# One of four weight products of an attention-and-MLP kernel, done by seven block products of halves

## The chip, the cores and the metric

The kernel runs on one core of one Trainium2 chip. The metric is the time of one execution on the device, in microseconds (us); smaller is better. The engines are named as in the profile: PE (TensorE, with PEld for its weight loads), DVE (VectorE), ACT (ScalarE), POOL (GpSimd) and SP (SyncE, which here issues nearly all transfers).

## The reference, cut to what matters

```python
scores = einsum('bhij,hg->bgij', scale * q @ k.T, w_pre)      # 4 batches, 12 heads, 448 rows, 64 wide
attn = softmax(scores);  attn = einsum('bhij,hg->bgij', attn, w_post)
x = (attn @ v)                                   # as 1792 tokens x 768
# first MLP:  w_in 768 x 2048, w_out 2048 x 768
h = x @ w_in;  g = relu(h) ** 2;                 x = g @ w_out
# second MLP: weights of its own, the same shapes
h = x @ w_in;  g = h * clip(h + 3, 0, 6) / 6;    out = g @ w_out
```

## The kernel before, in words

The four batches are worked off in two groups of two (`gi` 0 and 1). Each group goes through its attention and then through both MLPs, which work on the two batches at once: everything is held transposed, features along the 128 partitions and 2 x 448 tokens along the columns. `e` counts the two batches of the group.

Products are made at about full float32 accuracy out of fp32r matmuls: each operand is split in a high part (a copy in the rounded type, made by ACT) and a low part (the value less its high part), and one product is three matmuls: high by high, low weights by high data, high weights by low data. One matmul has a 128 x 128 block of weights and 448 columns of data.

An MLP is a list of units; a unit is one weight tile of 128 x 768. The 16 "h" units make the hidden values: unit `fc` gives 128 of the 2048 hidden features, for both `e`, in 2 x 18 matmuls (six blocks along the 768 features, three matmuls each). The 16 "p" units make the output in two halves (`dg` 0 and 1) of eight units, each 36 matmuls into six accumulators (three `d` of 128 features, two `e`), which stay open over the eight units. A group has thus 64 units. In the second group the weights come from DRAM (`kept`), where the first group has put them converted.

The order of the work on each engine is the order in which the program issues it; each engine works its list off in that order, and waits where an operand or a buffer is not ready. `Mlps.run` goes through the units: at the head of unit n it issues the load of unit n + 2 (SP) and `split(n + 1)`, that is `wh` of the next unit on ACT and `wl` behind it, on POOL in the second group. `wh` and `wl` have two buffers each, so `wh` of unit n + 1 needs the matmuls of unit n - 1 done. Then come the unit's matmuls. In an "h" unit `act` follows each product (for the second MLP: ACT makes `r` = relu(h/6 + 1/2), DVE makes `g` = min(r, 1) * h, both read the product where it lies), and `split_g` (ACT the high part, POOL the low part). The last of a unit's two products is taken up within the next unit: `act` before `split(n + 1)`, `split_g` behind it. At the end of the first MLP `finish` splits its output for the second: ACT makes `yh`, DVE `yl`.

PE's results lie in eight banks. In attention, and before the change in the MLPs too, they are four named tiles: `bs` and `bx`, two banks each, `bm` and `bo`, two single banks each; the allocation of this program puts `bs` in banks 0 and 1, `bx` in 2 and 3, `bm` in 4 and 5, `bo` in 6 and 7. `hidden` takes `bm`. Attention ends with `closing`, whose last products are read out of `bx` and then of `bs` (into `xr`, line 302).

The tile framework puts in the semaphore waits. Buffers with one tag take turns.

Of the kernel before, what the change touches and what calls it, by code (L numbers as in the profile page):

```python
# [7 lines left out]
F32 = mybir.dt.float32  # L8
F32R = mybir.dt.float32r
U32 = mybir.dt.uint32  # L10
I64 = mybir.dt.int64
# [26 lines left out]


# [19 lines left out]
def attention_mlp_kernel(ctx: ExitStack, tc, qT, kT, v, w_pre, w_post, mask, w1_in, w1_out, w2_in, w2_out, outT):  # L59
# [22 lines left out]
    ps = ctx.enter_context(tc.tile_pool(name="ps", bufs=2, space=PSUM))  # L82
# [372 lines left out]
    kept = {}  # L455

    class Mlps:
        def __init__(self, gi, att):
            self.gi, self.att = gi, att
            self.units = []  # L460
            for which, (w_in, w_out) in enumerate(((w1_in, w1_out), (w2_in, w2_out))):
                self.units += [("h", which, n, w_in[n]) for n in range(NF)]
                self.units += [("p", which, n, w_out[n // NU, n % NU]) for n in range(DG * NU)]
            self.W = w1_in.shape[-1]
            self.arena, self.ready, self.late, self.scaled = None, {}, [], set()
# [5 lines left out]
        def wr(self, n):  # L471
            at = 2 * 2 * self.W + self.W * (n % 3)
            return self.arena[:, at:at + self.W]

        def load(self, n):
            if n >= len(self.units):
                return
            if self.arena is None:
                self.arena = sh.tile([P, 7 * self.W], F32, tag="e1", name=f"arena{self.gi}")
            if self.gi == 0:  # L480
                nc.sync.dma_start(out=self.raw(n).bitcast(I64), in_=self.units[n][3])
            else:
                nc.sync.dma_start(out=self.wr(n), in_=kept[n])
# [71 lines left out]
        def hidden(self, which, fc, e, wh, wl):  # L555
            cols = slice(e * S, (e + 1) * S)
            hp = bank("bm", f"ps_h{self.gi}_{which}_{fc}_{e}")
# [38 lines left out]

        def opening(self):
# [6 lines left out]
        def run(self, mp, behind):  # L604

            rest = None
            for n, (kind, which, m, _) in enumerate(self.units):
# [11 lines left out]
                if kind == "p":  # L619
                    self.convert(n + 2, 1)  # L620
                wh, wl = self.ready.pop(n)
                if kind == "h":
# [23 lines left out]
                if u == 0:  # L646
# [10 lines left out]
                if m == 0 and which == 0:  # L657
                    self.yh = sh.tile([P, KC, T], F32R, tag="x1", name=f"yh{self.gi}")
                    self.yl = sh.tile([P, KC, T], F32R, tag="x2", name=f"yl{self.gi}")
                ends = u == NU - 1  # L660
                for e in range(NB):
                    self.project(u, e, wh, wl, acc)
                    if ends:
                        self.finish(which, dg, e, range(DB), acc)
                if which == 0 and m == DG * NU - 1:
# [7 lines left out]
    with tc.manual_schedule():  # L673
# [4 lines left out]
        for gi in range(groups):  # L678
# [10 lines left out]
            with tc.tile_pool(name=f"mp{gi}", bufs=1, reuse_waits="tile") as mp:  # L689
                mlp.run(mp, att.opening() + att.ahead() if att else [])  # L690
# [54 lines left out]
```

## Time and profile before

| | us |
|---|---|
| median of 3 runs | 1404.93 (1404.64 to 1406.46) |
| profiled execution, its own time | 1403.79 |
| its span, first to last instruction | 1401.9 |
| second group, first MLP, h units | about 931.3 to 1048.0 |
| second group, first MLP, p units | 1048.0 to 1165.0 |
| second group, second MLP, h units | 1165.0 to 1281.4 |
| second group, second MLP, p units | 1281.4 to the end |

The times of the stages are from the span's start. The span leaves out 1.9 us of the profiled execution's own time.

### The profile page before, as it was taken

Reading aid. Unit: us, or ns where it says so; the run is one execution under the profiler, and the core shown is the slowest. Engines: PE = TensorE matmul, PEld = TensorE weight load, DVE = VectorE, ACT = ScalarE, POOL = GpSimd, SP = SyncE. Lnnn points to the kernel's source line nnn. Section 1 sums busy time; section 2 is a strip of 40 time slices with the busy share of each in tenths; the row PEclk is TensorE's granted clock in tenths of the full one; section 3 lists DMA queues with packets and bytes.
Section 4 is the critical chain, followed back from the end, with each engine's and each line's share of the span. In section 5 each row is a group of like instructions: output and inputs, shape, how many; then the busy total and the mean of one; then the engine's idle time right before and its main releaser. Section 6 shows DMA issues by size and latency. Waiting matters only on the chain.

```text
span 1401.9 us, 22130 instructions
## 1 busy us (share of the span) xinstructions
PE 1385.5 (99%) x8500; PEld 1194.9 (85%) x8500; DVE 670.8 (48%) x1297; ACT 549.3 (39%) x1025; POOL 385.5 (27%) x431
## 2 busy tenths in 40 slices
PE   8999999999999999999999999999999999999998
PEld 3777778999989899988977777789999999999998
DVE  4777677877565687755547766741110102111000
ACT  4554445555222355524244534434431114443121
POOL 0222223344100133300012212245552224554221
PEclk9999999999999999999999999999999999999999
DMA  6453543555545455566554435311111111111121
GB/s 176 131 138 89 141 111 123 169 167 153 171 153 169 137 167 170 165 188 200 178 144 131 126 101 142 99 65 53 49 57 57 57 57 48 55 57 57 57 93 43
DMA packets 68366, 162.67 MB, mean 116 GB/s; under 512 B 6821, under 2 KB 43429, under 8 KB 68261
## 3 DMA queue, kind: packets, MB, share of 16 engines
q1 hardware_dynamic: 64805, 155.75, 38.0%
q10 hardware_dynamic: 3456, 5.51, 1.0%
q8 instruction: 67, 1.10, 0.3%
q14 instruction: 38, 0.31, 0.1%
HBM read 92.03 MB, written 30.67 MB: 88 GB/s over the span
## 4 chain that ended last, share of the span: by engine, by line
PE 95%; DVE 2%; ACT 1%; DMA 1%; issue 1%; POOL 0%; SPq 0%; ACTq 0%; POOLq 0%; DVEq 0%
PE ps_h L561 33%; PE ps_a L575 12%; PE bx L575 11%; PE ps_o L267 11%; PE bs L575 10%; PE ps_m L219 9%; PE bx L294 3%; PE bs L294 2%; PE bs L192 2%; PE bx L192 2%; DMA t<-s 0%; PE ps_s L307 0%; PE ps_s L192 0%; DVE arena L501 0%; DMA first<-in_dram 0%
## 5 line engine op out<-in xcount | busy, mean ns | idle before, releaser
L267 PEld LDWEIGHTS ps_o<-w2s,p 120*112 120x112 f32 (+1 forms) x1440 | 169.7, 177 | 70.9 <-issue 56.2
L517 ACT ACTIVATE wh<-arena 128x768 fp32r<-128x768 f32 x128 | 107.4, 839 | 294.4 <-PE bs L575 247.2
L236 ACT ACTIVATE p<-ps_m,mx 120x448 f32<-120x448 f32 x180 | 114.2, 634 | 186.2 <-DVE z L242 83.5
L519 POOL TENSOR_TENSOR wl<-arena,wh 128x768 fp32r<-128x768 f32 x64 | 118.2, 1847 | 236.3 <-ACT wh L517 233.1
L267 PE MATMUL ps_o<-w2s,p 120*112 120x120 f32 (+1 forms) x1440 | 181.2, 269 | 2.0 <-POOL w2s L256 1.8
L219 PE MATMUL ps_m<-t,w1f 120*120 120x448 f32 x360 | 168.2, 550 | 5.2 <-DMA t<-s 2.6
L256 POOL TENSOR_SCALAR w2s<-w2f,rz 120x120 f32<-120x120 f32 x180 | 66.4, 369 | 356.2 <-DVE rz L248 315.2
L553 POOL TENSOR_TENSOR gl<-g,gh 128x448 fp32r<-128x448 f32 x80 | 98.8, 1236 | 228.1 <-ACT gh L552 180.0
L561 PE MATMUL ps_h<-xh,wh 128*128 128x448 f32 x384 | 140.6, 366 | 0.0
L561 PE MATMUL ps_h<-xh,wl 128*128 128x448 f32 x384 | 140.3, 365 | 0.1
L561 PE MATMUL ps_h<-yh,wh 128*128 128x448 f32 x384 | 140.3, 365 | 0.0
L561 PE MATMUL ps_h<-yh,wl 128*128 128x448 f32 x384 | 140.2, 365 | 0.0
L561 PE MATMUL ps_h<-xl,wh 128*128 128x448 f32 x384 | 139.6, 364 | 0.1
L561 PE MATMUL ps_h<-yl,wh 128*128 128x448 f32 x384 | 139.4, 363 | 0.0
L282 DVE COPY a<-ps_o 112x480 f32<-112x480 f32 (+1 forms) x176 | 115.1, 654 | 31.8 <-PE ps_o L267 22.1
L228 DVE TENSOR_REDUCE mx<-ps_m 120x1 f32<-120x448 f32 x180 | 111.6, 620 | 23.2 <-PE ps_m L219 20.1
L519 DVE TENSOR_TENSOR wl<-arena,wh 128x768 fp32r<-128x768 f32 x64 | 62.8, 981 | 104.7 <-ACT wh L517 103.8
L575 PE MATMUL ps_a<-gh,wh 128*128 128x448 f32 x288 | 106.5, 370 | 0.0
L575 PE MATMUL ps_a<-gh,wl 128*128 128x448 f32 x288 | 104.8, 364 | 0.0
L542 DVE SCALAR_TENSOR_TENSOR g<-r,ps_h 128x448 f32<-128x448 f32 x64 | 39.7, 620 | 119.0 <-ACT r L541 115.9
L575 PE MATMUL bx<-gh,wh 128*128 128x448 f32 x256 | 93.4, 365 | 2.4 <-DVE yl L585 2.4
L575 PE MATMUL bx<-gh,wl 128*128 128x448 f32 x256 | 93.3, 364 | 0.0
(105 smaller groups left out, 2552.8 us busy)
## 6 DMA issues: line engine op xcount, KB each, us to landing
arena<-in_dram SPq DMA_DIRECT2D x64, 768.0 KB
t<-s SPq DMA_DIRECT2D x176, 210.0 KB
keep<-arena SPq DMA_DIRECT2D x64, 384.0 KB
arena<-keep SPq DMA_DIRECT2D x64, 384.0 KB
v<-in_dram SPq DMA_DIRECT2D x8, 672.0 KB
outT_dram<-ot ACTq DMA_DIRECT2D x24, 224.0 KB
kr<-in_dram SPq DMA_DIRECT2D x18, 224.0 KB
qr<-in_dram SPq DMA_DIRECT2D x30, 110.0 KB
```

The costliest lines, as they stand in the source:

```text
L219: nc.tensor.matmul(m[:rows, :S], lhsT=w1f.rearrange("p i g -> p (i g)")[:rows, :rows], rhs=self.live.pop(("t", i))[:rows], start=True, sto ...
L228: nc.vector.reduce_max(mx[:rows], m[:rows, :S], axis=AX.X, negate=True)
L236: nc.scalar.activation(pt[:rows], m[:rows, :S], AF.Exp, bias=mx[:rows], accum_out=z[:rows])
L256: nc.gpsimd.tensor_scalar(w2s[:rows, :G * ni].rearrange("p (g i) -> p g i", g=G), w2f[:rows, :, :ni], rz[:rows], 1.0, op0=ALU.mult, op1=AL ...
L267: nc.tensor.matmul(o[:JP, q * G * ni:(q + 1) * G * ni], lhsT=pt[:rows, q * JP:(q + 1) * JP], rhs=w2s[:rows, :G * ni], start=True, stop=True)
L282: nc.vector.tensor_copy(dst, src)
L294: nc.tensor.matmul(xo[e * D:(e + 1) * D, k * n:(k + 1) * n], lhsT=self.v[:, q, g, :], rhs=self.aa[c][:, q, g, :n], start=(q == 0), stop=(q ...
L517: nc.scalar.activation(wh, self.wr(n), AF.Copy)
L519: eng.tensor_tensor(out=wl, in0=self.wr(n), in1=f(wh), op=ALU.subtract)
L553: nc.gpsimd.tensor_tensor(out=gl, in0=g, in1=f(gh), op=ALU.subtract)
L561: nc.tensor.matmul(hp[:, :S], lhsT=lw[:, c * P:(c + 1) * P], rhs=rw[:, c, cols], start=(k == 0), stop=(k == 3 * KC - 1))
L575: nc.tensor.matmul(acc[d, e][:, :S], lhsT=lw[:, wc], rhs=rw[fc, e], start=(fc == 0 and k == 0), stop=(fc == NF - 1 and k == 2))
```

## The change

In the second group's second MLP the 16 "h" units are replaced by 28 "s" units. Take two hidden tiles (a "pair") as the rows, and the first and second half of the 768 features (384 each) as the columns of a 2 x 2 matrix A of weight blocks; the halves of x by the two batches `e` are the 2 x 2 matrix B. Their product is made with seven block products (the Winograd form) and sums of blocks. A product is three 128 x 128 blocks, nine matmuls, into one bank; an "s" unit holds two. Eight pairs make 56 products, worked off two pairs (14 products, seven units) at a time, in the order `PRODUCTS`. The numbers 1 to 7 name the products: 1 = A11 B11, 2 = A12 B21, 3 = S4 B22, 4 = A22 T4, 5 = S1 T1, 6 = S2 T2, 7 = S3 T3.

The sums of weights S1 to S4 are made on DVE during the first MLP's p units (`prepare`), and put into DRAM (`sums`). The sums of x, T1 to T4, and all their high and low parts are made where the first MLP's output is finished (`finish_mixed`; the branch in the diff is that of the last accumulators). Results are put together by DVE while they are read out of the banks (`combine`), and the gate follows one product later (`gate`). For hidden tiles 10 to 15 (`LATE`) the split of g is left to the first three p units (`split_late`). For this group's MLPs the four named bank tiles are closed and all eight banks become one pool `pb` that takes turns, from bank 0 on. Weight tiles from unit 16 on get three buffers of their own. `wl` of the s units and of the last p units is made by DVE instead of POOL. A scratch area in SBUF is made smaller.

```diff
+PRODUCTS = (
+    (1, 0), (1, 1), (2, 0), (2, 1), (6, 0), (7, 0), (5, 0), (4, 0), (3, 0), (6, 1), (7, 1), (5, 1), (4, 1), (3, 1),
+)
+SUMS = {6: 0, 3: 1, 7: 2, 5: 3}
+LATE = 10
...
+                if self.last and which == 1:
+                    self.base = at
+                    self.prods = [(p, 2 * j + i) for j in range(NF // 4) for p, i in PRODUCTS]
+                    self.units += [("s", which, n, None) for n in range(len(self.prods) // 2)]
...
         def load(self, n):
...
+                for i in range(2):
+                    p, pair = self.prods[2 * m + i]
+                    a = self.base + 2 * pair
+                    if p in SUMS:
+                        of = sums[pair][:, SUMS[p] * HW:(SUMS[p] + 1) * HW]
+                    else:
+                        of = kept[a + (p == 4)][:, (p > 1) * HW:(1 + (p > 1)) * HW]
+                    nc.sync.dma_start(out=self.wr(n)[:, i * HW:(i + 1) * HW], in_=of)
...
-            eng = nc.vector if self.gi == 0 else nc.gpsimd
+            eng = nc.vector if self.gi == 0 or self.last and n >= self.base else nc.gpsimd
             eng.tensor_tensor(out=wl, in0=self.wr(n), in1=f(wh), op=ALU.subtract)
...
+        def bank(self, tag, name):
+            if self.last:
+                return self.mb.tile([128, 512], F32, tag="pb", name=name, bufs=8)
...
+        def prepare(self, n):
...
+            nc.vector.tensor_tensor(out=a22, in0=a21, in1=a22, op=ALU.add)
+            nc.vector.tensor_tensor(out=a21, in0=a11, in1=a21, op=ALU.subtract)
+            nc.vector.tensor_tensor(out=a11, in0=a22, in1=a11, op=ALU.subtract)
+            nc.vector.tensor_tensor(out=a12, in0=a12, in1=a11, op=ALU.subtract)
+            sums[m] = dr.tile([P, 4 * HW], F32, name=f"sums{m}")
+            nc.sync.dma_start(out=sums[m], in_=self.pr.rearrange("p c f -> p (c f)"))
...
+        def part(self, hi, lo, src):
+            nc.scalar.activation(hi, src, AF.Copy)
+            nc.gpsimd.tensor_tensor(out=lo, in0=src, in1=f(hi), op=ALU.subtract)
...
+        def finish_mixed(self, dg, e, acc):
...
+            for d in range(DB):
...
+                elif e == 0:
...
+                else:
+                    t4 = self.t4[d]
+                    nc.vector.tensor_tensor(out=t1, in0=a, in1=t1, op=ALU.subtract)
+                    self.part(b2[:, 2], b2[:, 3], t1)
+                    nc.vector.tensor_tensor(out=t3, in0=a, in1=t3, op=ALU.subtract)
+                    self.part(b3[:, 0], b3[:, 1], t3)
+                    nc.vector.tensor_tensor(out=t4, in0=t4, in1=a, op=ALU.subtract)
+                    self.part(self.b4[0][d], self.b4[1][d], t4)
+                    nc.scalar.activation(b3[:, 2], a, AF.Copy)
+                    nc.vector.tensor_tensor(out=b3[:, 3], in0=a, in1=f(b3[:, 2]), op=ALU.subtract)
...
+        def combine(self, p, pair, a):
...
+            if p == 1:
...
+                nc.scalar.activation(self.u[1, pair], a, AF.Copy)
+                return None
+            if p in (6, 7):
...
+                add(self.u[p, pair], self.u[1 if p == 6 else 6, pair])
+                return None
...
+            add(g, self.u[{2: 1, 3: 6, 4: 7, 5: 7}[p], pair])
+            if p == 5:
+                add(self.u[6, pair], self.u[6, pair])
+            r = sh.tile([P, S], F32, tag="w0", name=f"rs{fc}_{e}", bufs=2)
+            nc.scalar.activation(r, g, AF.Relu, bias=half, scale=1.0 / 6.0)
+            return fc, e, r, g
+
+        def gate(self, fc, e, r, g):
+            nc.vector.scalar_tensor_tensor(out=g, in0=r, scalar=1.0, in1=g, op0=ALU.min, op1=ALU.mult)
+            if fc < LATE:
+                self.part(self.gh[fc, e], self.gl[fc, e], g)
...
+        def run(self, mp, behind, mb=None):
...
                 self.load(n + (3 if self.gi == 0 else 2))
...
+                if kind == "s":
...
+                    for i in range(2):
+                        if gate:
+                            self.gate(*gate)
+                        gate = self.combine(*self.product(2 * m + i, wh, wl))
+                    continue
...
+                if self.last and which == 1 and m < (NF - LATE) // 2:
+                    self.split_late(m)
...
+                    if ends and self.last and which == 0:
+                        self.finish_mixed(dg, e, acc)
...
+                att_banks.close()
+                with tc.tile_pool(name="mb", bufs=8, space=PSUM, reuse_waits="tile") as mb:
+                    mlp.run(mp, [], mb)
```

## Rows read from the trace of the kernel before

**Rows 1.** The page: busy time of each engine, share of the span, instructions.

```profile
PE 1385.5 (99%) x8500; PEld 1194.9 (85%) x8500; DVE 670.8 (48%) x1297; ACT 549.3 (39%) x1025; POOL 385.5 (27%) x431
```

**Rows 2.** The changed stage: stretch, length, busy PE PEld DVE ACT POOL, clock, DMA share, GB/s.

```profile
1165.00:1281.40 116.40, 116.40 (x577) 108.11 (x576) 19.89 (x32) 49.89 (x79) 64.85 (x47) 1.00 0.18 55
```

**Rows 3.** The chain that ended last: start, duration, what; the stage that is changed.

```profile
1164.96 116.47 PE ps_h L561 x576
```

**Rows 4.** Timeline: attention's end and the second group's first matmul, DVE and PE.

```profile
932.21 0.51 DVE L302 COPY xr<-bs 128x354 f32<-128x354 f32 x1
...
931.28 0.47 PE L561 MATMUL ps_h<-xh,wh 128*128 128x448 f32 x1
```

**Rows 5.** Groups by line and form, 870 to 1402 us: count, busy, mean ns.

```profile
L519 POOL TENSOR_TENSOR wl<-arena,wh 128x768 fp32r<-128x768 f32 x64 | 118.2, 1847 | 236.3 <-ACT wh L517 233.1 <-issue 3.2
L517 ACT ACTIVATE wh<-arena 128x768 fp32r<-128x768 f32 x64 | 53.7, 839 | 171.1 <-PE bs L575 126.8 <-PE ps_a L575 37.7 <-issue 6.2
L553 POOL TENSOR_TENSOR gl<-g,gh 128x448 fp32r<-128x448 f32 x40 | 46.4, 1159 | 17.5 <-ACT gh L552 14.2 <-DVE gh L550 3.4
L541 ACT ACTIVATE r<-ps_h,half 128x448 f32<-128x448 f32 x32 | 20.3, 635 | 54.2 <-PE ps_h L561 54.2
L552 ACT ACTIVATE gh<-g 128x448 fp32r<-128x448 f32 x32 | 18.5, 579 | 12.5 <-DVE g L542 12.1
L538 ACT ACTIVATE r<-ps_h 128x448 f32<-128x448 f32 x32 | 17.5, 546 | 64.4 <-PE ps_h L561 64.4
L585 DVE TENSOR_TENSOR yl<-ps_a,yh 128x448 fp32r<-128x448 f32 x4 | 2.5, 625 | 104.3 <-ACT yh L584 104.3
```

**Rows 6.** Timelines of ACT, DVE and POOL, one hidden product being taken up.

```profile
1168.64 0.64 ACT L541 ACTIVATE r<-ps_h,half 128x448 f32<-128x448 f32 x1 [2.37 <-PE ps_h L561]
...
1169.38 0.62 DVE L542 SCALAR_TENSOR_TENSOR g<-r,ps_h 128x448 f32<-128x448 f32 x1 [3.17 <-ACT r L541]
...
1170.03 0.58 ACT L552 ACTIVATE gh<-g 128x448 fp32r<-128x448 f32 x1 [0.76 <-DVE g L542]
```

**Rows 7.** Timelines of the first group: DVE and ACT instructions that follow without a wait.

```profile
445.38 0.96 DVE L519 TENSOR_TENSOR wl<-arena,wh 128x768 fp32r<-128x768 f32 x1 [3.27 <-ACT wh L517]
446.26 0.55 DVE L499 TENSOR_SCALAR arena<-arena 128x768 f32<-128x768 f32 x1
...
471.22 0.62 DVE L585 TENSOR_TENSOR yl<-ps_a,yh 128x448 fp32r<-128x448 f32 x1
471.75 0.61 DVE L585 TENSOR_TENSOR yl<-bx,yh 128x448 fp32r<-128x448 f32 x1
...
504.33 0.64 ACT L541 ACTIVATE r<-ps_h,half 128x448 f32<-128x448 f32 x1 [0.85 <-PE ps_h L561]
504.87 0.84 ACT L517 ACTIVATE wh<-arena 128x768 fp32r<-128x768 f32 x1
```

**Rows 8.** Timelines of POOL and DVE around 931 us.

```profile
930.15 0.62 DVE L530 TENSOR_TENSOR xl<-xr,xh 128x448 fp32r<-128x448 f32 x1 [0.64 <-ACT xh L528]
931.08 1.20 DVE L530 TENSOR_TENSOR xl<-xr,xh 128x448 fp32r<-128x448 f32 x1 [0.31 <-ACT xh L528]
...
930.66 1.15 POOL L530 TENSOR_TENSOR xl<-xr,xh 128x448 fp32r<-128x448 f32 x1 [1.80 <-ACT xh L528]
```

**Rows 9.** Timeline of ACT at the end of the first MLP of the second group.

```profile
1165.00 0.55 ACT L584 ACTIVATE yh<-bs 128x448 fp32r<-128x448 f32 x1 [0.68 <-DVE yl L585]
1165.44 0.83 ACT L517 ACTIVATE wh<-arena 128x768 fp32r<-128x768 f32 x1
```

**Rows 10.** The kernel's start: stretches as in rows 2, then PE's timeline.

```profile
16.00:18.00 2.00, 2.00 (x3) 0.80 (x4) 0.27 (x1) 0.00 (x0) 0.00 (x0) 0.50 0.53 131
18.00:20.00 2.00, 1.79 (x4) 0.28 (x2) 1.15 (x4) 0.89 (x3) 0.00 (x0) 0.76 0.56 146
...
15.88 3.26 PE L219 MATMUL ps_m<-t,w1f 120*120 120x448 f32 x4 [2.38 <-DMA t<-s]
```

**Rows 11.** Waits of SP's queue, 931 to 1402 us: total, times, longest.

```profile
SPq L483 <- POOL wl L519: 411.8, 60, 8.6
```

More of the change, by code (lines that the diff above doesn't have):

```diff
@@ L459, in __init__ @@
             self.gi, self.att = gi, att
[L460 removed]
+            self.last = gi > 0 and gi == B // NB - 1
+            self.units, at = [], 0
             for which, (w_in, w_out) in enumerate(((w1_in, w1_out), (w2_in, w2_out))):
[L462 to L463 removed]
+                if self.last and which == 1:
[3 more added lines that the diff above has]
+                else:
+                    self.units += [("h", which, n, (w_in[n], at + n)) for n in range(NF)]
+                at += NF
+                self.units += [("p", which, n, (w_out[n // NU, n % NU], at + n)) for n in range(DG * NU)]
+                at += DG * NU
             self.W = w1_in.shape[-1]
+            self.mp, self.own, self.u, self.gates = None, {}, {}, 0
             self.arena, self.ready, self.late, self.scaled = None, {}, [], set()
@@ new lines, in right, with product @@
+        def right(self, p):
+            t, k = {1: (self.b1, 0), 2: (self.b1, 2), 5: (self.b2, 0), 6: (self.b2, 2), 7: (self.b3, 0), 3: (self.b3, 2),
+                    4: (None, 0)}[p]
+            if p == 4:
+                return lambda d: (self.b4[0][d], self.b4[1][d])
+            return lambda d: (t[:, k, d, :], t[:, k + 1, d, :])
+        def product(self, k, wh, wl):
+            (p, pair), at, right = self.prods[k], k % 2 * HW, self.right(self.prods[k][0])
+            to = self.bank("pb", f"ps_s{p}_{pair}")
+            for d in range(DB):
+                wc = slice(at + d * P, at + (d + 1) * P)
+                bh, bl = right(d)
+                for j, (lw, rw) in enumerate(((wh, bh), (wl, bh), (wh, bl))):
+                    nc.tensor.matmul(
+                        to[:, :S], lhsT=lw[:, wc], rhs=rw, start=(d == 0 and j == 0), stop=(d == DB - 1 and j == 2))
+            return p, pair, to[:, :S]
@@ new lines, in gate, with split_late @@
+        def gate(self, fc, e, r, g):
+            nc.vector.scalar_tensor_tensor(out=g, in0=r, scalar=1.0, in1=g, op0=ALU.min, op1=ALU.mult)
+            if fc < LATE:
+                self.part(self.gh[fc, e], self.gl[fc, e], g)
+        def split_late(self, u):
+            if u == 0:
+                self.late_h = sh.tile([P, KC, T], F32R, tag="x1", name="late_h")
+                self.late_l = sh.tile([P, KC, T], F32R, tag="x2", name="late_l")
+            for fc in (LATE + 2 * u, LATE + 2 * u + 1):
+                for e in range(NB):
+                    cols = slice(e * S, (e + 1) * S)
+                    self.gh[fc, e], self.gl[fc, e] = self.late_h[:, fc - LATE, cols], self.late_l[:, fc - LATE, cols]
+                    self.part(self.gh[fc, e], self.gl[fc, e], self.late[:, fc - LATE, cols])
@@ L645, in run @@
                 alone = not behind and which == 1 and dg == DG - 1
-                if u == 0:
+                if u == 0 and self.last:
+                    acc = {(d, e): self.bank("pb", f"ps_a{self.gi}_{which}_{dg}_{d}_{e}")
+                           for e in range(NB) for d in range(DB)}
+                elif u == 0:
                     acc = {}
@@ L656, in run @@
                                 acc[d, e] = bank("bm", nm) if alone else bs[:, e, :]
-                if m == 0 and which == 0:
+                if m == 0 and which == 0 and not self.last:
                     self.yh = sh.tile([P, KC, T], F32R, tag="x1", name=f"yh{self.gi}")
@@ L662, in run @@
                     self.project(u, e, wh, wl, acc)
-                    if ends:
+                    if ends and self.last and which == 0:
+                        self.finish_mixed(dg, e, acc)
+                    elif ends:
                         self.finish(which, dg, e, range(DB), acc)
-                if which == 0 and m == DG * NU - 1:
+                if which == 0 and m == DG * NU - 1 and not self.last:
                     self.xh, self.xl = self.yh, self.yl
```

92 lines of the change are left out of this document (82 added, 10 removed).

## The prediction

> **What bounds the kernel now.** I read the page's busy times first. PE is busy for 99% of the span, no other engine for half of it [rows 1]. The chain of waits then says what a matmul is worth: the changed stage stands in it as one unbroken run of PE, 576 matmuls in 116.47 us [rows 3], 0.2022 us each. The table by stretch shows the same stage with DVE busy for 19.9 us of 116.4, ACT for 49.9, POOL for 64.9 [rows 2]. So today a matmul less is 0.2022 us less, as long as the other engines bring weights and data in time. Whether they still do is read from single instructions and from the order in which each engine has to take them.
>
> **What is removed.** Eight pairs by nine matmuls less: 576 become 504, and 72 x 0.2022 = 14.6 us of PE's work go.
>
> **Busy time of what comes in.** A round is two pairs, seven s units, 126 matmuls, 25.5 us of PE; there are four. Durations, each from the nearest row: `wl` on DVE 0.96, an add that reads a bank 0.62 (`yl` has the same operands), a gate 0.62 (`xl` unhindered, two operands in SBUF) [rows 5, 7, 8]; `wh` on ACT 0.84, `gh` 0.58, `gl` on POOL 1.16 [rows 5]. The relu now reads SBUF with a bias, which no row shows: `gh` from SBUF without one is 0.58, and the bias makes a relu out of a bank 0.635 instead of 0.546 [rows 5]; 0.58 + 0.09 = 0.67 is my estimate, 0.58 its lower bound. A round then has on DVE 7 `wl`, 14 adds and 8 gates, 20.4 us; on ACT 7 `wh`, 8 relus, 8 `gh` and 2 copies, 17.0 us; on POOL 8 `gl`, 9.3 us. All are below 25.5, so no engine becomes the bound by its busy time.
>
> **The order costs more.** Every s unit lasts 3.64 us on PE, half of an h unit, and has to bring a whole weight tile as before. DVE takes, in this order: `wl` of the next unit, the gate left over from the last product, the add of this unit's first product A, A's gate, the add of the second product B. A's gate waits for ACT's relu of A, and ACT takes `wh` of the next tile only behind the relu of B, which waits for the add of B. So from one `wl` to the next runs one chain through both engines. A following instruction without a wait can start some 0.09 us before the end of the one in front (0.88 after `wl`, 0.53 after an add, 0.54 after a relu of 0.64) [rows 7]; DVE hands over to ACT in 0.03 and a relu to DVE in 0.10 [rows 6]; I take 0.04 for the other hand-overs. With A and B both gated and no gate left over (second and fourth unit of a round):
> 0.88 `wl` + 0.62 add + 0.04 + 0.67 relu + 0.10 + 0.53 gate + 0.62 add + 0.04 + 0.57 relu + 0.84 `wh` + 0.04 = 4.95 us.
> The seventh unit (4, 3) has a gate left over as well: 5.48. The fifth (3, 6) needs no second relu, but `wh` stands behind `gh`: 0.88 + 0.53 + 0.62 + 0.04 + 0.67 + 0.10 + 0.62 + 0.04 + 0.49 + 0.84 + 0.04 = 4.87, or 3.9 where the split is put off (`LATE`). First, third and sixth unit have shorter chains (the third 2.9), so PE sets them, 3.64. PE wants a tile every 3.64 us and gets it later.
>
> **DVE behind POOL.** At 931.08 a DVE `xl` took 1.20 instead of 0.62: POOL had begun its own at 930.66, and DVE's ended 0.47 us after POOL's [rows 8]. Here `gl` of the gate left over runs until about 1.8 us behind that gate (`gh` 0.58, then 1.16), and A's gate comes 1.34 behind it (0.53 + 0.04 + 0.67 + 0.10): some 0.5 us more in the fifth and seventh unit, for hidden tiles below 10.
> A rule of the Trainium skill (SBUF — State Buffer, Who interferes with whom) says that a DVE instruction with two inputs in SBUF blocks against POOL for the whole instruction, while one with at most one SBUF input does not. For the gates the rows agree (1.20 against 0.62); for the adds no row shows an add under a POOL instruction. By the rule they cost nothing more; were they held as the gates are, 0.5 us in two units of three rounds would add an estimated 3 us.
>
> **Steady rounds.** Rounds two and three: 3.64 + 4.95 + 3.64 + 4.95 + 4.87 + 3.64 + 5.48 = 31.2, plus 2 x 0.5, less 0.8 that the third unit wins back: 31.4 each. Round four has no `gl`, its fifth unit 0.9 less, and the weights at the end of its last chain belong to a p unit that isn't due for another 7.28 us: 31.2 - 0.9 - 1.8 - 0.8 = 27.7.
>
> **The first round and the end of the first MLP.** Today three `yh` and `yl` close it and ACT is at `wh` 0.44 us behind the last `yh` [rows 9]. Now ACT has twelve instructions of `finish_mixed` for the last three accumulators, DVE twelve, POOL nine, all in front of `wh` and `wl` of the second s unit. Call PE's end of the p units E. DVE is through with the accumulators before at about E - 1.8. Per `d` it makes three subtractions, then waits for ACT's high part of T4 and the copy behind it, then makes the last low part: 0.53 + 0.53 + 0.62 + 0.04 + 0.49 + 0.55 + 0.04 + 0.53 = 3.33 us. Three make E + 8.2; ACT's last copy ends at E + 7.6 and `wh` at E + 8.4. PE has done the first s unit by E + 3.64 and waits 4.8 us. POOL's nine low parts run until about E + 9.5 and hold `wl` off until E + 10.5, which the unit's second matmul needs: the second unit ends at about E + 14.0 instead of 7.3. Five more with the excess of the chains of the fourth and fifth (1.3 + 1.2 + 0.5) make E + 35.2.
> Stage: 35.2 + 2 x 31.4 + 27.7 = 125.7 us against 116.5: 9.2 us longer.
>
> **The clock.** In the kernel's first microseconds PE waited 2.38 us; afterwards the granted clock was 0.50 from 16 to 18 us, the lower level of 1.2 GHz, and 0.76 over the next two [rows 10]. That is about 3 us of work at half speed, 1.5 us lost. A wait of 4.8 us may do the same: bounds 0 and 1.5, taken 0.8, because the second unit waits for `wl` anyway.
>
> **The banks.** `pb` begins at bank 0, which `bs` holds. If the framework lets it go only as a whole, the first matmul of this group's MLPs waits for the last read of `bs`, 932.21 + 0.51 = 932.72, instead of starting at 931.28 [rows 4]: 1.5 us. If it tracks banks, nothing, since attention's last product lies in the other half. I take 1.5: the tile is one allocation.
>
> **What I cost at nothing.** Loads: two of 192 KB each 3.64 us are about 106 GB/s instead of 55 [rows 2], and SP may issue them when `wl` of three tiles before is done, two units ahead; a round trip through DRAM of about that size kept PE waiting for 2.38 us at the start [rows 10]. SP does little but wait for `wl` (411.8 us [rows 11]). If that cover were gone, each late load would stop PE for its lateness. `prepare`: four DVE instructions, at most 2.5 us in 14.6; they may hold POOL's `wl` by as much, which is 1.85 us in 7.28. The first half of `finish_mixed` is followed by p units of 7.28 us, its queue on ACT and POOL is done within some 5. `split_late`: four ACT and four POOL instructions, 4.6 us of POOL in 7.28, five units ahead of their use. `wl` of the last p units on DVE is 0.96 for 1.85, hidden either way.
>
> **The sum.** Own time of the profiled execution 1403.8 + 9.2 + 0.8 + 1.5 = 1415.3; the median of the runs stands 1.1 above it, so I forecast **1416.5 us**. Bounds of the unknown: no hold by POOL anywhere -5 (the 0.5 in four units, 1.1 in the first round, and the waits that follow from them), relu at 0.58 -2, banks -1.5, clock -0.8 or +0.7, hand-overs of 0.08 instead of 0.04 +3, a restart of PE after each wait (0.47 instead of 0.36 for its first matmul [rows 4]) +2. The likeliest case's own range: 1408 to 1422.
>
> **Rivals.** (a) *The chain fits.* If the chain of a unit with two gates took 3.64 or less instead of 4.95, PE would go on unbroken. For it: busy times fit. Against: 1.3 us would have to come out of eleven terms that are nearly all read from rows. Only the first round's 6.7 would stay: 1404.9 - 14.6 + 1.5 + 6.7 = 1398.5, without it 1392. (b) *About even.* Shorter relus, no hold by POOL and a first round half as late give 1416.5 - 5 - 2 - 3.4 = 1406. (c) *The clock falls in every round.* PE now waits in four units of seven; at 1.5 to 3 us a round more, 1423 to 1428. Against: the waits are about 1.3 us each, and the row shows the fall behind 2.38.
>
> **Chances.** Forecast 0.58, (a) 0.14, (b) 0.13, (c) 0.15. A change of 0.2%, 2.8 us, is about what a measurement can tell: faster below 1402.1, slower above 1407.7. (b) lies mostly within: faster 0.15, same 0.11, slower 0.74. The range takes in the forecast, (b), the slow end of (a) and the near half of (c): 1400 to 1426.
>
> **What would show it.** 504 matmuls in the stage, and PE idle ahead of the second, fourth, fifth and seventh unit of a round, with `wh` or `wl` as releaser; one wait of 4 to 6 us about 3.6 us behind the end of the first MLP; gates of about 1.1 us where POOL is at `gl`; a first matmul about 1.5 us later behind attention. It is wrong if PE runs unbroken through the s units, or if the longest waits there are for a load.

## The result and the profile after

The changed kernel took 1419.92 us in the median of four runs (1419.58 to 1420.34), beside 1405.7 of the kernel before on the same chip. The ratio is 1.0102, with a 95% interval of 1.0084 to 1.0119: slower by 1%. The forecast was 1416.5, its own range 1408 to 1422. The profiled execution took 1419.72 us, its span 1417.9. One execution of a run below took 1711.87 us at a mean granted clock of 0.752 and is left out of that run's figures.

First the page's busy times and the table by stretch for the changed stage (columns as in [rows 2]).

```profile
PE 1380.5 (97%) x8428; PEld 1183.2 (83%) x8428; DVE 781.1 (55%) x1441; ACT 568.3 (40%) x1060; POOL 342.4 (24%) x411
...
1168.00:1297.60 129.60, 111.55 (x506) 96.16 (x505) 84.40 (x124) 62.08 (x98) 32.97 (x29) 0.96 0.29 90
```

PE has 72 matmuls less than in [rows 1], as the change says, and the kernel is longer all the same. The changed stage lasts 129.5 us instead of the 116.5 of [rows 3]. No other engine is the bound by its busy time: DVE, the busiest of them, works for 84.4 of 129.6 us.

The chain of waits of the same execution (start, duration, what):

```profile
934.62 116.72 PE ps_h L593 x576
1051.34 109.61 PE ps_a L607 x540
1168.86 1.64 ACT b L654 x3
...
1178.27 2.01 DVE wl L551
1180.32 3.37 PE ps_s L713 x8
1202.56 1.90 PE ps_s L713 x8
...
1275.50 22.29 PE ps_s L713 x107
1297.78 116.68 PE ps_a L607 x576
```

Before, the stage was one line of PE. Now the chain leaves PE at the end of the first MLP (from 1161 to 1180 it runs through DVE and ACT), and again in each round; the last 107 matmuls of the s units are one unbroken line again. What PE waited for most between 925 and 1420 us, with total, times and longest:

```profile
PE ps_s L713 <- ACT wh L549: 11.5, 8, 6.4
PE ps_s L713 <- DVE wl L551: 6.6, 10, 1.3
PE ps_h L593 <- DVE xr L310: 1.5, 1, 1.5
```

All waits of the changed stage are for the two halves of a weight tile, none for a load. They come to 18.1 us. The rest of what is lost is inside PE's busy time: 504 matmuls one behind the other would take 504 x 0.2022 = 101.9 us, the row of the stage shows 111.55. That is the lower clock, which the stage shows at two places, and matmuls that start alone behind a wait.

The end of the first MLP, DVE, ACT, POOL and PE in order of time; `E`, the end of its p units, is at 1168.09:

```profile
1162.77 0.55 DVE L646 TENSOR_TENSOR pr<-pr 128x384 f32<-128x384 f32 x1
...
1164.54 0.56 DVE L649 TENSOR_TENSOR pr<-pr 128x384 f32<-128x384 f32 x1
...
1168.21 0.61 DVE L688 TENSOR_TENSOR t<-ps_a,t 128x448 f32<-128x448 f32 x1
...
1169.52 9.93 POOL L655 TENSOR_TENSOR b<-t,b 128x448 fp32r<-128x448 f32 x9 [13.05 <-ACT b L654]
...
1172.03 0.62 DVE L690 TENSOR_TENSOR t<-ps_a,t 128x448 f32<-128x448 f32 x1
...
1177.40 0.83 ACT L549 ACTIVATE wh<-wr 128x768 fp32r<-128x768 f32 x1
...
1178.27 2.87 DVE L551 TENSOR_TENSOR wl<-wr,wh 128x768 fp32r<-128x768 f32 x2
...
1178.29 0.74 PE L713 MATMUL ps_s<-b,wh 128*128 128x448 f32 x1 [6.44 <-ACT wh L549]
...
1180.32 0.74 PE L713 MATMUL ps_s<-b,wl 128*128 128x448 f32 x1 [1.29 <-DVE wl L551]
```

DVE has the four sums of `prepare` (L646 to L649) ahead of `finish_mixed`, so it comes to the last accumulators at E + 0.1. `wh` of the second s unit ends at E + 10.1, and PE, which was through with the first unit at E + 3.8, waits 6.44 us and then 1.29 for `wl`. The stretches around it:

```profile
1178.00:1180.00 2.00, 0.74 (x1) 0.29 (x1) 1.89 (x2) 1.84 (x4) 1.45 (x2) 0.50 0.01 4
1180.00:1182.00 2.00, 1.68 (x5) 1.51 (x6) 1.14 (x2) 0.00 (x0) 0.00 (x0) 0.50 0.31 77
1182.00:1184.00 2.00, 2.00 (x7) 1.78 (x6) 0.22 (x1) 0.00 (x0) 0.00 (x0) 0.53 0.84 250
1184.00:1190.00 6.00, 6.00 (x32) 5.56 (x31) 3.63 (x7) 3.28 (x6) 1.17 (x1) 1.00 0.09 30
```

The granted clock is 0.50 (1.2 GHz) from the end of the wait until about 1184. PE was busy for 0.74 + 1.68 + 2.00 = 4.4 us of that, so about 2.2 us are lost.

In the steady state, DVE's `wl` of seven units in a row shows the chain:

```profile
1237.40 0.96 DVE L551 TENSOR_TENSOR wl<-wr,wh 128x768 fp32r<-128x768 f32 x1 [1.00 <-ACT wh L549]
1243.29 0.96 DVE L551 TENSOR_TENSOR wl<-wr,wh 128x768 fp32r<-128x768 f32 x1 [1.53 <-ACT wh L549]
1247.03 0.96 DVE L551 TENSOR_TENSOR wl<-wr,wh 128x768 fp32r<-128x768 f32 x1 [2.24 <-ACT wh L549]
...
1252.01 0.96 DVE L551 TENSOR_TENSOR wl<-wr,wh 128x768 fp32r<-128x768 f32 x1 [1.53 <-ACT wh L549]
1254.68 0.95 DVE L551 TENSOR_TENSOR wl<-wr,wh 128x768 fp32r<-128x768 f32 x1
1259.65 0.96 DVE L551 TENSOR_TENSOR wl<-wr,wh 128x768 fp32r<-128x768 f32 x1 [1.53 <-ACT wh L549]
1264.91 1.26 DVE L551 TENSOR_TENSOR wl<-wr,wh 128x768 fp32r<-128x768 f32 x1 [0.84 <-ACT wh L549]
1268.97 0.96 DVE L551 TENSOR_TENSOR wl<-wr,wh 128x768 fp32r<-128x768 f32 x1 [1.00 <-ACT wh L549]
```

From start to start these are 5.89, 3.74, 4.98, 2.67, 4.97, 5.26 and 4.06 us, for a seventh unit and the first to sixth of the next round: 31.57 in all, where PE's own work is 25.5. DVE waits for ACT's `wh` ahead of nearly each, and ACT made that `wh` only behind the relu of the unit's second product.

### The profile page after: what moved, and what is told of

Its sections match the earlier page's. It is cut to its first block, busy times and chain, and to the rows that moved or that the text cites. A ratio compares the mean times of both kernels' runs of the same rounds, so it can differ in the third digit from the quotient of the medians.

```text
span 1417.9 us, 22298 instructions
## 1 busy us (share of the span) xinstructions
PE 1380.5 (97%) x8428; PEld 1183.2 (83%) x8428; DVE 781.1 (55%) x1441; ACT 568.3 (40%) x1060; POOL 342.4 (24%) x411
## 4 chain that ended last, share of the span: by engine, by line
PE 88%; DVE 5%; ACT 4%; issue 2%; DMA 1%; POOL 0%; SPq 0%; ACTq 0%; POOLq 0%; DVEq 0%
PE ps_h L593 24%; PE ps_a L607 21%; PE ps_o L275 11%; PE ps_m L227 9%; PE bx L607 5%; PE bs L607 5%; PE ps_s L713 3%; PE bx L302 3%; PE bs L302 2%; PE bs L200 2%; PE bx L200 2%; ACT wh L549 1%; DVE wl L551 1%; DVE gs L745 1%; PE ps_s L315 1%
## 5 line engine op out<-in xcount | busy, mean ns | idle before, releaser
L585 POOL TENSOR_TENSOR gl<-g,gh 128x448 fp32r<-128x448 f32 x60 | 75.6, 1260 | 214.3 <-ACT gh L584 165.9
L551 DVE TENSOR_TENSOR wl<-wr,wh 128x768 fp32r<-128x768 f32 x44 | 45.3, 1032 | 135.8 <-ACT wh L549 135.3
L607 PE MATMUL ps_a<-gh,wh 128*128 128x448 f32 x320 | 118.2, 369 | 0.0
L607 PE MATMUL ps_a<-gh,wl 128*128 128x448 f32 x320 | 116.5, 364 | 0.0
L549 ACT ACTIVATE wh<-arena 128x768 fp32r<-128x768 f32 x80 | 67.0, 838 | 123.3 <-PE bs L607 120.4
L549 ACT ACTIVATE wh<-wr 128x768 fp32r<-128x768 f32 x60 | 50.4, 839 | 164.4 <-PE ps_a L607 155.2
L713 PE MATMUL ps_s<-b,wh 128*128 128x448 f32 x336 | 100.3, 376 | 11.5 <-ACT wh L549 11.5
L582 DVE CAST gh<-g 128x448 fp32r<-128x448 f32 x64 | 39.8, 622 | 103.3 <-ACT g L571 103.3
L713 PEld LDWEIGHTS ps_s<-b,wh 128*128 128x128 f32 x336 | 65.0, 193 | 19.7 <-ACT wh L549 14.5
L570 ACT ACTIVATE r<-ps_h 128x448 f32<-128x448 f32 x64 | 34.8, 544 | 111.3 <-PE ps_h L593 111.3
L593 PEld LDWEIGHTS ps_h<-xh,wh 128*128 128x128 f32 x384 | 72.1, 188 | 7.4 <-issue 1.9
```

The lines of the kernel that those rows point to most:

```text
L585: nc.gpsimd.tensor_tensor(out=gl, in0=g, in1=f(gh), op=ALU.subtract)
L593: nc.tensor.matmul(hp[:, :S], lhsT=lw[:, c * P:(c + 1) * P], rhs=rw[:, c, cols], start=(k == 0), stop=(k == 3 * KC - 1))
L607: nc.tensor.matmul(acc[d, e][:, :S], lhsT=lw[:, wc], rhs=rw[fc, e], start=(fc == 0 and k == 0), stop=(fc == NF - 1 and k == 2))
L713: nc.tensor.matmul(to[:, :S], lhsT=lw[:, wc], rhs=rw, start=(d == 0 and j == 0), stop=(d == DB - 1 and j == 2))
```

## The experiments

The theory: PE is held by the chain wl, add, relu, gate, add, relu, wh, wl through two in-order queues, and at the hand-over by the finish of the last accumulators. The rivals: POOL's hold on DVE is what makes it too long; the hand-over alone, with the clock behind it, is the loss; the wait on the bank. Each run's ratio is to the kernel before on the same chip, whose medians lay between 1405.15 and 1406.05.

### The bank (two runs)

```diff
                 with tc.tile_pool(name="mb", bufs=8, ...) as mb:
+                    for k in range(4):
+                        mb.tile([128, 512], F32, tag="pb", name=f"skip{k}", bufs=8)
                     mlp.run(mp, [], mb)
```

> Four banks are skipped, so that the first product of the second group's MLPs lands in bank 4 (bm) instead of bank 0 (bs). Theory: the first matmul waits for bs as one allocation, 1.50 us by the profile of after; the wait goes and nothing takes its place: 1.5 us less than 1419.9, 1418.4, PE without a wait at the first hidden product. Rival: the wait only hides a later one, since the split of attention's last output (ACT, DVE, POOL) is needed 3.6 us later anyway: 1419.9.

1419.89 us, ratio 1.0098 (1.0081 to 1.0115). The opening wait of 1.5 us on DVE's `xr` was there as before, so tiles that nothing writes seem to have taken no bank. So this run is a repeat of the changed kernel and tells nothing of the bank. In the next run five tiles have a column written each:

```diff
+                    for k in range(5):
+                        skip = mb.tile([128, 512], F32, tag="pb", name=f"skip{k}", bufs=8)
+                        nc.vector.memset(skip[:, :1], 0.0)
```

> As e1, but five banks are taken by a one-column memset on DVE each, so that they are really given out and the first product lands in bank 4 (bm). Theory: the wait of 1.5 us ahead of the first matmul of the second group's MLPs goes: 1418.4, to be read from the profile. Rival: it comes back within the first two products, since the split of attention's output ends later: 1419.9.

1418.73 us, 1.0094 (1.0078 to 1.0109). PE's timeline of this run at the first product:

```profile
928.59 2.64 PE L302 MATMUL bx<-a,v 112*64 112x118 f32 x48 [0.58 <-ACT a L288]
...
933.58 0.47 PE L593 MATMUL ps_h<-xh,wh 128*128 128x448 f32 x1
```

The first product now follows `bx` by 4.99 us; in the changed kernel it is 934.62 - 928.05 = 6.57, with the 1.50 of wait in it. The wait is gone, so it did hang on the bank; the gain of 1.2 us in the medians is within the intervals. The bank was a small term.

### Another order on DVE and ACT

The second product's combine is taken up behind the next unit's split, and the gate of the first stays in front of the split after that:

```diff
-                    for i in range(2):
-                        if gate:
-                            self.gate(*gate)
-                        gate = self.combine(*self.product(2 * m + i, wh, wl))
+                    if held:
+                        gate = self.combine(*held)
+                    first = self.combine(*self.product(2 * m, wh, wl))
+                    if gate:
+                        self.gate(*gate)
+                    held = self.product(2 * m + 1, wh, wl)
+                    gate = None
+                    if first:
+                        self.gate(*first)
...
```

> Only the order of issue in the s units is changed: the second product of a unit is taken up behind the split of the next unit's weights instead of ahead of it, and its gate one product later. Nothing is left out. Theory (the chain through ACT and DVE): the waits for wh and wl from the third unit on (10.3 us in the profile of after, and about 0.1 us for each of 17 restarts) go, the wait of about 7.7 us at the second unit stays: 1407 to 1409. Rival (DVE held by POOL): holds stay where they are, 3 us less at the most, 1417. Rival (loads late): no change, 1420.

1420.19 us, 1.0097 (1.008 to 1.0114): a miss, no gain at all. The rival of late loads had the same time, but PE waited for no load here: its waits were 12.7 us for `wl` (14 times) and 7.0 for `wh` (3 times). The timeline of DVE and ACT over one unit:

```profile
1216.64 1.28 DVE L551 TENSOR_TENSOR wl<-wr,wh 128x768 fp32r<-128x768 f32 x1 [1.38 <-ACT wh L549]
1217.84 0.61 DVE L720 TENSOR_TENSOR gs<-ps_s,u 128x448 f32<-128x448 f32 x1
...
1218.55 0.67 ACT L741 ACTIVATE rs<-gs,half 128x448 f32<-128x448 f32 x1 [1.51 <-DVE gs L720]
1219.25 0.62 DVE L745 SCALAR_TENSOR_TENSOR gs<-rs,gs 128x448 f32<-128x448 f32 x1 [0.80 <-ACT rs L741]
1219.91 0.58 ACT L654 ACTIVATE ghs<-gs 128x448 fp32r<-128x448 f32 x1 [0.69 <-DVE gs L745]
1220.39 0.83 ACT L549 ACTIVATE wh<-wr 128x768 fp32r<-128x768 f32 x1
...
1221.26 1.27 DVE L551 TENSOR_TENSOR wl<-wr,wh 128x768 fp32r<-128x768 f32 x1 [1.38 <-ACT wh L549]
```

The loop has only closed over other links: wl, add, relu, gate, gh, wh, wl, in 4.62 us where PE has 3.64 us of work. `wh` still stands behind something that needs this unit's `wl`, so this reordering changed the links and not the loop.

### A shorter finish

Of the last accumulators' finish only T2 is made first; T3, T4 and the parts of B22 follow in the first two s units:

```diff
                     nc.vector.tensor_tensor(out=t1, in0=a, in1=t1, op=ALU.subtract)
                     self.part(b2[:, 2], b2[:, 3], t1)
-                    nc.vector.tensor_tensor(out=t3, in0=a, in1=t3, op=ALU.subtract)
...
+                    self.left.append((d, a))
...
+                if kind == "s" and m < 2:
+                    self.finish_left(m)
```

> Only the end of the first MLP is changed: behind the last accumulators just T2 is made and split; T3 follows behind the split of the second s unit's weights, T4 and the parts of B22 behind that of the third. Nothing is left out. Theory: wh of the second unit no longer stands behind twelve instructions, the wait of 6.4 + 1.3 us and the half-speed stretch behind it (some 2.6 us) go but for about 1 to 2 us: 1410 to 1412. Rival: the same work is due soon after, and the wait moves to the third or fourth unit: 3.6 us less at the most, 1416.

1419.28 us, 1.0095 (1.008 to 1.011): the rival was right that the wait only moves, and 0.6 us less than the changed kernel is within the intervals. Two of PE's waits in the first units:

```profile
1176.79 0.47 PE L720 MATMUL ps_s<-b,wl 128*128 128x448 f32 x1 [1.15 <-DVE wl L551]
1185.18 0.74 PE L720 MATMUL ps_s<-b,wh 128*128 128x448 f32 x1 [4.62 <-ACT wh L549]
```

The wait of 6.44 us became 0.61 and 1.15, and then 4.62 two units later, behind the work that was put off. The granted clock was 0.50 from 1184 to 1190.

### Sums, finish, order together

The two edits above with the sums of weights two units earlier (and the tiles that took no bank):

```diff
-            if not self.last or not NF <= n < NF + DG * NU:
+            if not self.last or not NF - 2 <= n < NF - 2 + DG * NU:
```

> The three changes of the runs before together (banks, order in the s units, end of the first MLP), and the weights' sums made two units earlier. Nothing is left out. Theory: PE runs through the 504 matmuls with 1 to 2 us of waits: 1405.7 - 14.6 + 1 to 2 = 1392 to 1393. Rivals: POOL's holds and late loads stay, 1398 to 1405.

1417.0 us, 1.0079 (1.0064 to 1.0094): a miss by 24 us, for the reason of the run on the order: the loop was still closed (PE waited 12.4 us for `wl`, 15 times). So a new theory of the cure was needed: not another order within a unit, but `wh` taken out of the loop.

### High parts two units ahead

ACT makes `wh` of unit n + 2 at the head of unit n, with a third buffer for it in the memory of `pr`; loads are issued three units ahead; combine and gates of the second product come behind the next unit's split. The sums stand two units earlier and the finish is the short one.

```diff
+                self.split_high(n + 2)
                 self.split(n + 1)
...
+                    if held:
+                        gates.append(self.combine(*held))
+                    if m:
+                        self.gates_of(gates)
+                    gates.append(self.combine(*self.product(2 * m, wh, wl)))
+                    if m:
+                        self.gates_of(gates)
+                    held = self.product(2 * m + 1, wh, wl)
...
```

> Weights two tiles ahead: wh of unit n + 2 is issued on ACT, wl of unit n + 1 on DVE, at the head of unit n (a third wh buffer, in the memory of the weights' sums), and only behind them the last product of unit n - 1 is taken up and the gates follow. So no wh stands on ACT behind anything that waits for this unit's wl. With it the shortened end of the first MLP and the weights' sums two units earlier. Nothing is left out. Theory (one chain wl, add, relu, gate, gh, wh, wl closes in every unit; the order of e2 left it closed, at 4.6 us a unit): with the chain open PE runs nearly unbroken through the s units, 1405.7 - 14.6 + 1.5 (first matmul) + 2 to 4 of waits, 1394 to 1398. Rival (DVE held by POOL, 20 us of DVE in 25 us): 1405 to 1412. Rival (loads late): 1417.

1395.43 us (1394.49 to 1398.97), 0.9935 (0.9922 to 0.9947): faster than both kernels, as expected. Its stage by stretch, PE's waits there, and the group of `wl` in the steady part (1190 to 1274; count, busy, mean ns, idle before):

```profile
1168.00:1274.00 106.00, 104.13 (x507) 96.05 (x506) 89.69 (x124) 62.33 (x98) 41.62 (x29) 0.98 0.34 105
...
PE ps_s L733 <- DVE wl L564: 1.9, 1, 1.9
...
L564 DVE TENSOR_TENSOR wl<-wr,wh 128x768 fp32r<-128x768 f32 x24 | 28.7, 1195 | 10.9 <-PE ps_s L733 8.7 <-ACT rs L761 1.4 <-ACT ghs L667 0.5
```

And the group of `wl` in the changed kernel, 1200 to 1274 us:

```profile
L551 DVE TENSOR_TENSOR wl<-wr,wh 128x768 fp32r<-128x768 f32 x16 | 16.6, 1036 | 19.3 <-ACT wh L549 19.2
```

There, 19.2 of 19.3 us of DVE's idle time ahead of `wl` were for `wh`; here none is, and most of what is left is for PE. PE waits once, 1.9 us, instead of 18 times. The stage is 105.8 us (1168.21 to 1274.0), of which 101.9 are matmuls. And `wl` itself takes longer than before, 1195 ns against 1036: in the open loop DVE's instructions beside POOL got longer, and PE shows no wait for it.

### What POOL's part is worth (two runs)

In the first, `wl` of the s units, and of the last p units, goes back from DVE to POOL:

```diff
-            eng = nc.vector if self.gi == 0 or self.last and n >= self.base else nc.gpsimd
+            eng = nc.vector if self.gi == 0 else nc.gpsimd
```

> One part undone: wl of the s units and of the last p units is made by POOL again (1.85 us instead of 0.96). Nothing is left out. Theory: DVE's add of the first product no longer stands behind wl, 0.9 us out of each unit's chain, but wl itself ends 0.9 us later behind wh, and POOL has 22 of 25 us a round: 1412 to 1418. Rival (busy time of DVE sets the stage): 45 of wl leave DVE, 1405 or less.

1416.03 us, 1.0078 (1.0065 to 1.0092). PE waited 10.2 us for `wl`, 15 times, now on POOL, and 4.5 at the hand-over. With the 28 `wl` of the stage taken off DVE the kernel is 3.9 us below the changed one (3.3 when each is set against the kernel before on its chip): the loop goes over POOL instead and still doesn't fit.

In the second, POOL's low parts of hidden tiles 0 to 9 are left out, and the high parts stand in for them:

```diff
-                self.part(self.gh[fc, e], self.gl[fc, e], g)
+                nc.scalar.activation(self.gh[fc, e], g, AF.Copy)
+                self.gl[fc, e] = self.gh[fc, e]
```

> The low part gl of the gated values of hidden tiles 0 to 9 in the s units is left out (POOL does nothing there; the p units read the high part in its place, the same number of matmuls). Theory: only the holds by POOL go, some 0.3 to 0.4 us in each gated unit of three rounds and in two or three wl a round: 4 to 6 us less, 1414 to 1416, and the waits for wh stay. Rival (POOL's holds are what makes PE wait): the waits from the third unit on go, 1408.

1417.07 us, 1.0086 (1.0073 to 1.01), 2.9 less than the changed kernel, or 2.3 when each is set against the kernel before on its chip; the intervals overlap, and the 4 to 6 us that were expected were not there. PE's waits say the same: 9.5 us for `wh` and 5.7 for `wl` are left, 15.2 of 18.1. The holds are small: the rival that made them the cause is out.

### The bank in the faster version

The run with high parts ahead, and the five written tiles of the run on the bank.

> The version with the high parts two units ahead (1395.4 us), with the first matmuls of the second group's MLPs moved to a bank whose last read lies earlier, as in the run on the bank (opening wait 1.5 us gone there). Theory: the opening wait is a pure addition to the end: 1393.5 to 1394.5 us, no wait on DVE xr at the first product, the rest of the trace as in that version. Rival: the start of the first MLP is set by the finish of attention anyway and the time stays at 1395 to 1396 us.

1393.29 us (1391.48 to 1394.62), 0.991 (0.9897 to 0.9923): 0.2 us below what the theory had, and the fastest version here, 12.6 us below the 1405.87 of the kernel before beside it. PE's waits from 925 us on have no line for `xr` any more, and the one for `wl` is the same 1.9. Behind it the granted clock stayed at 1.00 here, where in the version before it had fallen to 0.50, so the 2.1 us between the two medians need not all be the bank's.

### The hand-over, one part at a time (three runs)

First the high parts ahead alone, with the sums at their old place and the long finish.

> High parts two units ahead and combine and gates behind them, but the sums of weights at their old place and the finish of the last accumulators as in the changed kernel. Theory (two separate losses, a closed chain in the units and a late finish): the units run without waits from the third s unit on, and the hand-over keeps a wait on the low part of the second s unit's weights, since DVE reaches it only behind the finish: about E + 11 us, that is a wait of 5.5 to 7 us and some 3 us at the lower clock after it; 1401 to 1404 us. Rival (the hand-over costs little by itself, its wait matters only through the chain): 1395 to 1398 us.

1414.54 us, 1.0062 (1.0049 to 1.0074): outside the range of the theory and that of the rival. The chain of waits says why:

```profile
1168.98 3.66 PE ps_s L726 x18
1173.03 3.64 DMA pr<-keep
```

The third `wh` buffer takes turns with `pr`. With the sums at their old place, the last load of `pr` has to wait until PE is through with the first s unit, and the finish stands behind it in DVE's queue; PE waited 7.7 and 12.2 us. The run shows a new dependence that this edit makes, not the price of the hand-over. Behind it, its s units ran without a wait.

Then high parts ahead and the sums two units earlier, with the long finish.

> As the run with the high parts two units ahead alone, and the sums of weights two units earlier, so that DVE's last four of them (2.3 us) no longer stand ahead of the finish. Theory: the wait at the hand-over is shorter by 2 to 2.3 us (about 4 us) and the stretch at the lower clock shorter too: 2 to 4 us faster than that run, 1398 to 1401 us. Rival (the last sums were not what held the finish): no difference to that run.

1399.61 us, 0.996 (0.9948 to 0.9972). The absolute time is as expected; the difference of 14.9 to the run above is the buffer's doing. PE's one wait in the s units:

```profile
1178.38 0.74 PE L726 MATMUL ps_s<-b,wl 128*128 128x448 f32 x1 [5.24 <-DVE wl L564]
```

Against the version with the short finish that is 4.2 us more (3.5 when each is set against the kernel before beside it), 3.4 of them wait (5.24 against 1.87): once the loop is open, the long finish costs some 4 us by itself. In the changed kernel the same cut gained 0.6, within the intervals.

Last, the changed kernel with nothing else but the sums two units earlier.

> The changed kernel with one thing else: the sums of weights are prepared two units earlier in the first MLP's second stage, so that the last four additions of DVE (2.3 us) no longer stand between its low part of the weights and the finish of the accumulators. Theory (this is the step of the prediction that was mis-sized): the finish reaches the last accumulators at about E - 2 instead of E + 0.1, the first high part of the second s unit ends at about E + 8 instead of E + 10.1, the wait at the hand-over falls from 6.4 to about 4.3 us and the time by 2 to 3 us, 1416.5 to 1418 us; the waits in the later rounds stay as they are. Rival (ACT's or POOL's own work sets that high part): wait still over 6 us, 1419 to 1420.5 us.

1416.82 us, 1.0083 (1.0069 to 1.0096), 3.1 less than the changed kernel and as expected; the intervals overlap, so the trace has to say what it gained. DVE, ACT and PE at the hand-over, with E at 1167.84:

```profile
1166.03 0.62 DVE L688 TENSOR_TENSOR t<-ps_a,t 128x448 f32<-128x448 f32 x1
...
1175.22 0.83 ACT L549 ACTIVATE wh<-wr 128x768 fp32r<-128x768 f32 x1
...
1176.11 0.47 PE L713 MATMUL ps_s<-b,wh 128*128 128x448 f32 x1 [4.51 <-ACT wh L549]
1177.10 0.74 PE L713 MATMUL ps_s<-b,wl 128*128 128x448 f32 x1 [0.53 <-DVE wl L551]
```

DVE comes to the last accumulators at E - 1.8, `wh` ends at E + 8.2, and the wait is 4.51 us. With the sums out of the way the hand-over is the one that the prediction had worked out (E - 1.8, E + 8.4, 4.8).

## Why the prediction was right, and where it was off

The mechanism was right and is shown: the time lay in the order, not in busy times. Between the last two runs of the hand-over, 1416.82 and 1399.61, both with the early sums and the long finish, only the reading ahead and what goes with it differ: it took out 17.2 us without taking any work off an engine. That edit has two parts, the early `wh` (with its third buffer and earlier loads) and the combines and gates put off; no run has one of them alone, so which of the two does it is not shown.

The start of a round is counted back from its second unit: the start of that unit's first matmul, less the wait ahead of it, less one s unit (3.64 us); in round two of the changed kernel 1211.24 - 1.21 - 3.64 = 1206.39. So the rounds compare, in us:

| | predicted | changed kernel | sums two units earlier |
|---|---|---|---|
| first round | 35.2, and 0.8 for the clock | 38.3 | 35.2 |
| second | 31.4 | 32.05 | 32.1 |
| third | 31.4 | 31.6 | 31.6 |
| fourth | 27.7 | 27.6 | 27.6 |
| stage | 126.5 | 129.5 | 126.5 |

The equal totals in the first and last column are in part luck: the 35.2 measured has the clock's loss in it, so it is 0.8 below the forecast, and rounds two and three are 0.7 and 0.2 above it.

**The steady chain** held where it was worked out. Two gates and none left over: 4.95 predicted, 4.98 and 4.97 measured. The fifth unit with POOL's hold: 4.87 + 0.5 = 5.37, measured 5.26. The seventh: 5.48 + 0.5 = 5.98, measured 5.89. The relu from SBUF with a bias, which no row of before showed, took 0.67, as estimated. Rivals (a) and (b) fell with this: every chain of two gates is over 3.64.

Three things came otherwise. The first unit took 3.74 us and the sixth 4.06, where the prediction let PE set 3.64; in the sixth POOL held `wl` itself, 1.26 us instead of 0.96, and the prediction had priced that hold for the gates alone. PE waited at the second, fourth, sixth and seventh unit of round two, not at the fifth that was named. And round four is luck: the sum has long chains behind its second and fourth unit, but PE waited only at its second (0.84 and 0.52 us) and then ran on unbroken, since `wl` of the third tile came 1.60 us behind the one before it, where rounds two and three have 3.73 and 3.74.

**POOL's hold.** Groups of the changed stage (mean ns in the third field):

```profile
L720 DVE TENSOR_TENSOR u<-ps_s,u 128x448 f32<-128x448 f32 x24 | 14.8, 615 | 0.4
L745 DVE SCALAR_TENSOR_TENSOR gs<-rs,gs 128x448 f32<-128x448 f32 x20 | 14.4, 718 | 7.1 <-ACT rs L741 7.1
...
L745 DVE SCALAR_TENSOR_TENSOR late<-rs,late 128x448 f32<-128x448 f32 x10 | 6.2, 621 | 2.7 <-ACT rs L741 2.7
```

Gates of hidden tiles below 10 take 718 ns in the mean, late ones, with no `gl` of their own, 621. Five of the twenty were held and came to 0.99 to 1.05 us, not to the 1.1 that the prediction named. Operations with one operand in a bank were not held: those of L690 at 1172.03 and 1175.32 took 0.62 and 0.61 us while POOL worked from 1169.52 to 1179.45, and `wl`, with two in SBUF, begun at 1178.27, ended at 1180.28, only behind POOL. By the rule of the Trainium skill (SBUF — State Buffer, Who interferes with whom) a DVE instruction with at most one input in SBUF doesn't contend with POOL; the trace agrees, and the 3 us that the adds might have cost were not there. Without POOL's low parts the kernel was 2.3 to 2.9 us faster; the prediction's bound was 5.

**The first round** is the term that was too small: 38.3 against 36.0. `prepare` was costed at nothing, since its four DVE instructions fit in 14.6 us of PE. The last four, 2.3 us, stood in DVE's queue ahead of `finish_mixed`, where the prediction had DVE free at E - 1.8; it came at E + 0.1. From there each step held (3.29 us per `d` where 3.33 was worked out, the first `wh` 10.0 behind the finish's start instead of 10.2). With the sums moved, the first round is 35.2, 3.1 less; a part of that is the clock, which was back at 1.00 by about 1180 there, not 1184.

**The clock** was taken as 0.8, at most 1.5; the rows give about 2.2 at the hand-over, above that bound. It did not fall in each round (rival (c)): between 1200 and 1214, with waits of 0.49, 0.83, 1.21 and 0.53 us, the granted clock was 1.00. But it fell once more, in round three, behind waits of 1.23 and 0.53 us:

```profile
1246.00:1248.00 2.00, 2.00 (x7) 1.80 (x6) 0.97 (x2) 0.99 (x2) 0.62 (x1) 0.50 0.34 126
```

The second unit of that round took 6.10 us from start to start, instead of 4.51 in round two. PE then found the fourth unit's tile ready, for which it had waited 0.21 and 0.53 us in round two, so the round was no longer for it. The first run on the bank, a repeat of this kernel, shows the same: there the clock fell in round two and not in round three, and the second units of rounds two, three and four start 32.05 and 31.21 us apart, here 32.07 and 31.19. Where the chain sets the pace, a slower PE cost the stage nothing.

**The bank** was 1.5 and measured 1.50. **Loads** kept nobody waiting, as costed.

**The sum.** The profiled execution is 4.4 us above the 1415.3 that the sum gave: 3.0 in the stage, and 1.8 since the second group's MLPs began 934.62 - 931.28 = 3.34 later, of which the bank is 1.50; 0.4 less elsewhere. Of those 1.8 us, 1.6 are of the kernel's beginning, whose code the change leaves as it is: PE's first wait for `t` ended at 17.50 instead of 15.88 [rows 10], and at times between 15.87 and 17.82 in the profiles of this case.

## What to carry to other kernels

Busy times that fit say nothing about a chain that goes through two in-order queues: add up one turn of it, from an operation to the same operation for the next tile, and compare that with the bound engine's work per tile. If the turn is longer, another order of the same links need not help (the one tried here did not open the loop); take one operation out of the loop by making it a tile or two earlier, and look at what its extra buffer takes turns with. And an edit that is hidden by its length may still stand in a queue ahead of something that isn't.

## What the runs showed of the hardware

PE's waits as the profile lists them were 18.1 us, while the stage lost 27.6 (129.5 less 101.9). The rest was in the busy time: the lower clock at two places, and matmuls that start alone, 0.47 us where those in a row come every 0.20.

Behind waits of 4.5 to 6.4 us the granted clock was 0.50 and came back to 1.00 some 4 to 9 us after the wait's end; after the same wait of 6.44 us this took 5.6 us in the changed kernel and 7.8 in its repeat. The length of a wait did not decide alone whether the clock fell: after the one of 1.87 us in the faster version it was 0.67 from 1182 to 1184 and 0.50 from 1184 to 1186, after one of 1.86 us in the version with the bank it stayed at 1.00. Waits of 1.21 and 0.53 us, one matmul apart, left it at 1.00 in round two of the changed kernel, and those of 1.23 and 0.53 us in round three were followed by 0.50.

With four PSUM tiles that nothing writes ahead of it, the first product waited 1.51 us for the old bank as before; with five that had one column written each, it did not wait.
